# One loop body rewritten: 64x64 products gathered into three runs, a flip moved ahead, a first block of a sum changed

## The chip, the cores and the metric

The kernel runs on one core of a Trainium2 chip. A core has five engines with a queue each, which run side by side and wait for one another by semaphores: TensorE (PE in the profile; PEld is its weight load), VectorE (DVE), ScalarE (ACT), GpSimd (POOL) and SyncE (SP), which here only issues transfers. The metric is the device time of one execution in microseconds (us). Three executions of the kernel before took 638.33, 639.71 and 641.10 us; the median is 639.71 us.

## What is computed

The first block is a recurrent attention with 4 batches, 8 heads, 768 tokens and 40 dimensions of a head. Its state is a 40 by 40 matrix for each batch and head:

```
for t in range(S):
    y[:, :, t] = einsum('bhd,bhde->bhe', rt, state)
    Sa = einsum('bhde,bhe->bhd', state, at)
    state = state * wt - einsum('bhd,bhe->bhde', Sa, bt) + einsum('bhd,bhe->bhde', vt, kt)
```

Its output, as 3072 rows of 320, goes through the second block:

```
h = x @ w_in                                  # 320 -> 1024
sm = exp(h - max(h)) / (sum(exp(h - max(h))) + 1e-9)
solu = h * sm
ln = (solu - mean(solu)) / sqrt(var(solu) + 1e-6) * g_ln
out = ln @ w_out                              # 1024 -> 320
```

The attention's inputs are 32-bit floats. The three weights come as 64-bit floats, which the kernel reads as integers and takes apart on the chip.

## The kernel before

**Chunks.** The sequence is cut into chunks of 64 tokens. Two batches make a pair, so a step covers 2 x 64 tokens on 128 partitions; there are 2 pairs x 12 chunks = 24 such steps, numbered i. Within a chunk the recurrence is solved in closed form: a 64 by 64 triangular system for each head is inverted, and the rest is products.

**The products.** Most of them are 64 by 64 or smaller. They use a quarter of TensorE's array each: `half(p)` picks 64 rows and 64 columns, and `in_turn` deals the 16 products of a step (2 batches x 8 heads) over the four quarters. One name in the profile is 16 such products: `pu` (the solve), `pnt`, `pl`, `ps` (the scores, two runs of 16), `py`, `pz`, `px` (two runs), `pyo` (one run from the state, then 32 products of 104 columns). In 32-bit floats one product shows as two records. All go through the helper `mm`, so their line is L254 and one tells them by the tile's name. Between them stand full-width operations: transposes (`pa`, `pb`, `pk`, `pv`, `pr`, `pst`, `pei`, `plnT`), the running sum `pcum`, the product with w_in (`h`, six matmuls, two of them on 64 rows each) and the product with w_out (`po`, two groups of four).

**fence().** It is a TensorE drain: nothing is issued until all earlier products have ended. It stands where two row halves of the array would add into the same PSUM bank (within `px` and within `pyo`).

**The loop** (L785 to L843) runs i from -1. A pass does different things for different steps: step j = i + 5 gets its inputs scaled, transposed and multiplied (`front`, `norm`); step i + 1 gets its scores (`scores`), the coupling of its inverted blocks (`couple`, `close`); step i is solved and read out (`solved`, `answered`, `read`, `leave`); the second block works on steps i - 2, i - 3 and i - 4 (`hidden`, `exped`, `weighed`, `spreadof`, `folded`, `output`). The order in the text is the order in each engine's queue for PE, DVE, POOL and SP; only ScalarE's order is chosen by the scheduler.

**The inversion.** Every second pass two chunks' triangular blocks are inverted on VectorE in 30 steps of two instructions each (`prod`, then `uu`; L415 and L417). `some(n)` puts n of these steps at its place in the queue. The way there: `norm` writes `nt` to DRAM (POOL queue), four `blk` transfers bring it back in another layout (POOL queue), the steps run, the result `uu` goes to DRAM (SP queue), and `bring` fetches it as `tu` and `uh` (SP). `flip` transposes `tu` on VectorE; `py` needs that.

**Buffers.** PSUM tiles come from three pools. `banks` (two buffers of two banks) holds pu, ps, py, pnt, pl, pz, pyo, px in turn; `bank` (two buffers of one bank) holds the transposes, pcum, po and plnT in turn; `h` has one buffer. A tile that takes a buffer waits until its holder two places before has been copied out.

**The weights** are taken apart by `split`, in 13 parts: two VectorE instructions, three on ScalarE, then three on VectorE. `narrow(n, steps)` does n parts and spreads inversion steps between. Two parts come before the loop, the rest in passes -1 to 3. A pass 4 subtracts the mean from w_out (`centred`).

## Time and profile before

| | us |
|---|---|
| median of three executions | 639.71 |
| the profiled execution | 639.79 |
| its span, first to last instruction | 637.70 |
| TensorE busy | 567.5 (89%) |
| VectorE busy | 461.9 (72%) |
| GpSimd busy | 269.1 (42%) |
| ScalarE busy | 245.3 (38%) |
| start of pass 0 (its `px`) | 71.03 |
| start of pass 5 | 188.11 |
| start of pass 17 | 457.91 |
| end of pass 23's attention | 594.46 |

Passes 5 to 16 take 22.48 us each, pass 17 takes 21.95, pass 18 takes 21.37 and passes 19 to 22 take 19.78 each, from `px` to `px`. A busy time counts an instruction from its start to its modelled end, so for TensorE the distance from one start to the next is the better measure of what a piece costs. An idle time in brackets names what ended it. The chain of work that ended last gives PE 71% of the span and DVE 13%.

### The profile page before, as it was taken

How to read it: one execution, taken by the hardware profiler on the slowest of the kernel's cores; microseconds unless marked ns; L12 is line 12 of the kernel's file. 1: busy time of each engine (PE TensorE's matmuls, PEld its weight loads, DVE VectorE, ACT ScalarE, POOL GpSimd, SP SyncE). 2: the span in 40 equal slices, each digit the busy share in tenths (PEclk: the TensorE clock that was granted, in tenths of full speed). 3: DMA queues.
4: the chain of work that ended last, by engine and by line, in shares of the span. 5: the costliest groups of instructions: out<-in, count | busy, mean ns of one | idle time of the engine just before them, and what ended most of it. 6: DMA issues, size and time to landing. Idle time of an engine off the chain costs nothing.

```text
span 637.7 us, 26729 instructions
## 1 busy us (share of the span) xinstructions
PE 567.5 (89%) x11451; PEld 399.6 (63%) x11451; DVE 461.9 (72%) x1286; ACT 245.3 (38%) x498; POOL 269.1 (42%) x444
## 2 busy tenths in 40 slices
PE   5245677988999999999999999999999999999995
PEld 3134555756577677667667767666776666766653
DVE  4678799999878778778878777787887796443431
ACT  3412545554334434433443443344243333332221
POOL 3334345574274444445543642743544642222200
PEclk9665676688999999999999999999999999999998
DMA  8939896474355535544554553654423422210000
GB/s 166 159 73 169 170 164 131 107 152 87 71 110 93 111 87 95 107 93 103 103 120 79 108 116 73 119 107 95 91 53 70 98 49 49 51 36 26 24 20 21
DMA packets 217868, 59.92 MB, mean 94 GB/s; under 512 B 203216, under 2 KB 213048, under 8 KB 217752
## 3 DMA queue, kind: packets, MB, share of 16 engines
q1 hardware_dynamic: 200984, 34.47, 31.7%
q0 software_dynamic: 11376, 19.25, 12.6%
q10 hardware_dynamic: 5392, 4.51, 2.5%
q8 instruction: 90, 1.47, 1.0%
q14 instruction: 26, 0.21, 0.1%
HBM read 40.10 MB, written 13.37 MB: 84 GB/s over the span
## 4 chain that ended last, share of the span: by engine, by line
PE 71%; DVE 13%; DMA 6%; issue 4%; ACT 2%; SPq 2%; POOL 1%; DVEq 0%; ACTq 0%; POOLq 0%
PE h L254 16%; PE po L703 14%; PE pyo L254 7%; PE px L254 4%; PE pu L254 3%; DVE uu L417 3%; PE plnT L692 3%; PE ps L254 3%; DVE prod L415 3%; PE pl L254 2%; PE pr L334 2%; PE pnt L254 2%; PE pk L334 2%; PE pa L334 2%; PE pz L254 2%
## 5 line engine op out<-in xcount | busy, mean ns | idle before, releaser
L254 PE MATMUL h<-w_in,xT 128*128 128x512 f32 (+1 forms) x288 | 121.6, 614 | 0.0
L415 DVE TENSOR_TENSOR prod<-blk,uu 128x30 f32<-128x30 f32 (+4 forms) x360 | 99.0, 275 | 24.0 <-DMA blk<-nt_dram 14.0
L703 PE MATMUL po<-w,lnT 128*128 128x320 f32 x384 | 113.5, 440 | 0.0
L417 DVE TENSOR_TENSOR uu<-uu,prod 128x30 f32<-128x30 f32 (+4 forms) x360 | 101.9, 283 | 12.4
L703 PEld LDWEIGHTS po<-w,lnT 128*128 128x128 f32 x384 | 70.5, 190 | 29.3 <-issue 2.3
L655 DVE TENSOR_REDUCE nmax<-h 128x1 f32<-128x1024 f32 x24 | 29.4, 1224 | 60.0 <-PE h L254 59.9
L388 POOL DMA_DIRECT2D nt_dram<-nt x20 | 18.3, 916 | 119.0 <-DVE nt L362 97.7
L254 PEld LDWEIGHTS h<-w_in,xT 128*128 128x128 f32 (+1 forms) x288 | 38.9, 190 | 21.9 <-issue 20.8
L623 POOL TENSOR_TENSOR st<-tot,ex 104x160 f32<-104x160 f32 x44 | 22.1, 520 | 70.4 <-DVE tot L619 68.2
L681 POOL TENSOR_TENSOR rs<-c,mhalf 128x1 f32<-128x1 f32 x24 | 13.4, 559 | 91.0 <-DVE c L680 89.6
L635 POOL DMA_DIRECT2D xT<-x x96 | 48.7, 512 | 0.0
L254 PE MATMUL pyo<-lv,kb 64*64 64x104 f32 x768 | 38.6, 274 | 6.0 <-DVE lv L362 3.3
L693 ACT COPY lnT<-plnT 128x512 f32<-128x512 f32 x48 | 26.1, 589 | 43.3 <-PE plnT L692 43.3
L399 POOL DMA_DIRECT2D blk<-nt_dram x42 | 33.3, 800 | 13.0 <-DMA nt_dram<-nt 12.7
L658 ACT ACTIVATE e<-h,nmax 128x1024 f32<-128x1024 f32 x24 | 26.8, 1115 | 28.6 <-DVE nmax L655 27.5
L254 PE MATMUL pyo<-lu,kb 64*64 64x104 f32 x768 | 37.2, 266 | 0.0
L664 DVE TENSOR_TENSOR e<-h,e 128x1024 f32<-128x1024 f32 x24 | 29.4, 1225 | 10.1 <-ACT e L658 10.1
L276 POOL DMA_DIRECT2D raw_r<-in_r_dram x48 | 34.9, 729 | 0.3 <-issue 0.3
L672 DVE BATCH_NORM_STATS2 bs<-e 128x6 f32<-128x512 f32 x48 | 30.9, 686 | 0.8
L707 ACT ACTIVATE osb<-po,rs 128x320 f32<-128x320 f32 x24 | 12.7, 528 | 48.5 <-PE po L703 29.6
L254 PEld LDWEIGHTS pnt<-aT,bT 40*64 40x64 f32 x768 | 14.6, 144 | 26.5 <-issue 25.0
L254 PEld LDWEIGHTS pyo<-lv,kb 64*64 64x64 f32 x768 | 23.9, 145 | 11.3 <-issue 7.7
(130 smaller groups left out, 1127.0 us busy)
## 6 DMA issues: line engine op xcount, KB each, us to landing
blk<-nt_dram POOLq DMA_DIRECT2D x42, 128.0 KB, 4.2
nt_dram<-nt POOLq DMA_DIRECT2D x20, 256.0 KB, 3.5
raw_w<-in_w_dram SPq DMA_DIRECT2D x48, 80.0 KB
a<-in_a_dram SPq DMA_DIRECT2D x48, 80.0 KB
raw_r<-in_r_dram POOLq DMA_DIRECT2D x48, 80.0 KB, 3.3
lv<-in_v_dram SPq DMA_DIRECT2D x48, 80.0 KB
out_dram<-osb ACTq DMA_DIRECT2D x24, 160.0 KB
raw_b<-in_b_dram SPq DMA_DIRECT2D x44, 80.0 KB
```

Source lines behind the costliest of these rows:

```text
L254: nc.tensor.matmul(o, lhsT=lhsT, rhs=rhs, start=start, stop=stop, skip_group_check=True)
L276: queue.dma_start(out=x[half(p), :, 0:D], in_=ap[2 * bp + p, :, ci * C:(ci + 1) * C, :].rearrange("h t d -> t h d"))
L334: nc.tensor.transpose(out=t[0:W2, j * P:(j + 1) * P], in_=x[:, 2 * j:2 * j + 2].rearrange("p a b -> p (a b)")[:, 0:W2], identity=ident)
L399: queue.dma_start(out=nb[home:home + Q], in_=blocks[n][:, Q * e:Q * e + Q, Q * e:Q * e + Q])
L415: nc.vector.tensor_tensor(out=t, in0=nb[:, j:j + 1, j + 1:Q].to_broadcast([P, n_c, m]), in1=u[:, 0:n_c, j:j + 1].to_broadcast([P, n_c, m]) ...
L417: nc.vector.tensor_tensor(out=u[:, 0:n_c, j + 1:Q], in0=u[:, 0:n_c, j + 1:Q], in1=t, op=ALU.subtract)
L635: nc.gpsimd.dma_start(out=xT[to:to + Q, 2], in_=x[at + P - 3 * D:at + D, 2])
L655: nc.vector.tensor_reduce(out=nmax, in_=d["h"], axis=AX.X, op=ALU.max, negate=True)
L658: nc.scalar.activation(out=e, in_=d["h"], func=AF.Exp, bias=nmax, accum_out=d["esum"])
L664: nc.vector.tensor_tensor(out=d["e"], in0=d["h"], in1=d["e"], op=ALU.mult)
L672: nc.vector.bn_stats(out=bs[:, x], in_=d["e"][:, x * 512:x * 512 + 512])
L703: nc.tensor.matmul(d["out"][:, 0:DM], lhsT=d["lnT"][:, f, :], rhs=w2[:, f, :], start=f == 0, stop=f == NF - 1)
```

## The change

Nothing that is computed changes, and no product is added. The order of the loop body changes, with the buffer counts of two tiles.

- **Three runs.** TensorE's 64x64 products stand in three places of a pass: `pu, pu, ps, ps`; `py, pnt, pl`; and `pz, pyo, px` with the two 64-row matmuls of `h` in it. `scores(i + 1)` moves behind `solved(i)`, `couple` ahead of `norm` and `answered`, and `px` of step i + 1 (`carried`, `driven`) into the end of pass i, between and behind the parts of `pyo`. The transposes `pk`, `pv`, `pr` of step i + 2 move from the middle of pass i + 1 to the end of pass i; `pst` stays with step i.
- **One fence** stands where there were two: behind the own half of `pyo`, the state part of `px` and the 64-row matmuls.
- **The sum for h** begins with its third block (64 rows each) at the end of a pass and ends with the second block in the next, so that maximum and exponential (`exped`) follow it and `weighed` comes behind `answered`.
- **VectorE's order.** `flip` stands behind the maximum and ahead of `nt` and `lu`; before it stood behind `lu`. `psi` and `lv` move to the start of the pass. The inversion's 15 steps of a pass are split 3, 5, 3, 4 (before 3, 6, 0, 6), and in passes 0 to 3 4, 4 or 5, 3, 4.
- **GpSimd's order.** `by_value` moves ahead of the write of `nt`.
- **Before the loop** attention inputs of step 0 are transposed and scored early; `bring(0)`, `bring(1)` and `load_values(1)` are issued ahead of the weights' `land(3)`; the steps are split differently.
- `narrow` begins all its parts, runs the steps, then ends all parts. The tile `scale` gets two buffers, the tile `s` one in place of two.
- `centred` stands behind `decay`, just ahead of `output`.

```diff
@@ narrow @@
+        begun = []
         for x in range(n):
             load, part = next(parts)
-            rest = split(*part)
-            next(rest)
-            some(n_steps // n + (x < n_steps % n))
+            begun.append((load, part, split(*part)))
+            next(begun[-1][-1])
+        some(n_steps)
+        for load, part, rest in begun:
             for _ in rest:
                 pass
@@ driven @@
-        if d["opened"]:
-            fence()
@@ read @@
-        else:
-            fence()
@@ hidden @@
-            if (kt, x) == (0, 0):
+            if (kt, x) == (NK - 1, 0):
...
-               start=kt == 0, stop=kt == NK - 1)
+               start=kt == NK - 1, stop=kt == NK - 2)
@@ before the loop @@
         front(i)
+        front_b(i)
         decay(i + 1)
+        some(4 * (i > 1))
         norm(i)
...
-            some(8)
+            some(4)
...
     by_value(0)
+    attend_kv(0)
+    attend_r(0)
...
+    load_keys(6, "w")
+    some(10)
+    scores(0)
     decay(5)
-    load_keys(6, "w")
-    land(3, nc.sync)
-    some(14)
     load_keys(5, "ba")
-    load_values(1)
     bring(0)
     bring(1)
+    load_values(1)
+    land(3, nc.sync)
@@ the loop @@
-    shares = {-1: (0, 6, 2, 6), 0: (0, 6, 4, 6), 1: (0, 6, 3, 6), 2: (0, 6, 3, 6), 3: (0, 6, 3, 6)}
-    narrowed = {-1: (0, 1), 0: (1, 1), 1: (1, 2), 2: (1, 2), 3: (1, 1)}
+    shares = {-1: (0, 10, 2, 2), 0: (4, 5, 3, 4), 1: (4, 4, 3, 4), 2: (4, 4, 3, 4), 3: (4, 4, 3, 4)}
+    narrowed = {-1: (1, 0), 0: (1, 1), 1: (1, 2), 2: (1, 2), 3: (1, 1)}
...
-        pieces = shares.get(i, (3, 6, 0, 6))
+        pieces = shares.get(i, (3, 5, 3, 4))
```

The body of a pass after the change, whole:

```
        bring(i + 1); load_values(i + 2); some(pieces[0])
        solved(i); scores(i + 1)
        load_keys(j + 3, "w"); load_keys(j + 2, "bak")
        stated(i); front(j)
        hidden(m - 2, ((0, 1),)); narrow(some_weights[0], pieces[1])
        front_b(j); decay_turned(j + 1)
        hidden(m - 2, ((1, 1),)); exped(m - 2)
        scaled(j + 1); left(i - 1); by_value(i + 2); decay(j + 2)
        if i == 3 + LAG: centred(mean, 6)
        output(m - 3, 0)
        flip(i + 1); some(pieces[2]); couple(i + 1); norm(j); answered(i)
        weighed(m - 2); spreadof(m - 2)
        if ok(j) and j % GRP == GRP - 1: begin_inverse(j // GRP)
        output(m - 3, 1); narrow(some_weights[1], pieces[3])
        close(i + 1); read(i, True); carried(i + 1)
        if ok(m - 1): hidden(m - 1, ((2, 0), (2, 1)))
        fence(); read(i, False); driven(i + 1)
        leave(i); folded(m - 2)
        hidden(m - 1, ((0, 0),)); attend_kv(i + 2)
        hidden(m - 1, ((1, 0),)); attend_r(i + 2)
```

Here m = i - 1. `attend_r` and `stated` are the two halves of the former `attend_rs` (rT; pst and s), and `front_b` is the last line of the former `front` (pb and bT).

## The prediction

> **What bounds the kernel now.** I read the page's busy shares and slices first, then busy time by stage.
>
> ```profile
> PE 567.5 (89%) x11451; PEld 399.6 (63%) x11451; DVE 461.9 (72%) x1286; ACT 245.3 (38%) x498; POOL 269.1 (42%) x444
> ...
> PE   5245677988999999999999999999999999999995
> ...
> PEclk9665676688999999999999999999999999999998
> ```
> ```profile
> 71.03:188.11 117.08, 97.71 (x2186) 74.19 (x2182) 106.43 (x290) 53.79 (x114) 61.88 (x94) 0.84 0.63 123
> 188.11:457.91 269.80, 267.15 (x5785) 188.39 (x5784) 209.40 (x600) 110.96 (x227) 131.87 (x217) 1.00 0.50 100
> ```
> The second view has length, then busy PE, PEld, DVE, ACT, POOL, clock, DMA share, GB/s. Up to 188 us VectorE bounds (106.43 of 117.08 in passes 0 to 4). From 188.11 on PE does: 267.15 of 269.80, at full clock, and the waits list shows no wait of PE there. Twelve passes of 22.48 us are a pure sum of PE pieces. So the third view is PE's timeline of such a pass (start, length):
>
> ```profile
> 300.53 0.68 PE L254 MATMUL px<-st,aT 40*64 40x40 f32 x32
> 301.31 0.68 PE L254 MATMUL px<-lv,psi 64*64 64x40 f32 x32
> 301.92 0.65 PE L334 MATMUL pa<-cst,a 128*104 128x128 f32 x4
> ...
> 302.84 1.02 PE L254 MATMUL h<-w_in,xT 128*128 128x512 f32 x2
> 303.79 0.69 PE L254 MATMUL pu<-tu,x 64*64 64x64 f32 x32
> 304.31 0.63 PE L254 MATMUL pu<-x,tu 64*64 64x40 f32 x32
> 304.86 0.65 PE L334 MATMUL pk<-cst,kb 128*104 128x128 f32 x4
> ...
> 305.78 1.02 PE L254 MATMUL h<-w_in,xT 128*128 128x512 f32 x2
> 306.74 0.69 PE L254 MATMUL pnt<-aT,bT 40*64 40x64 f32 x32
> 307.36 0.64 PE L334 MATMUL pr<-cst,r 128*104 128x128 f32 x4
> ```
> Start to start, pnt alone takes 0.62 us, pu's two runs 1.07, and (in the same view) ps, ps, py 1.53: 0.46 a run, and about 0.16 left over for leaving the mode. An h matmul costs 0.86 before another h and 0.95 before a 64x64 run: 0.09 for entering. **A slot costs 0.25 us beside its runs.** The two px start 0.78 apart where pu's start 0.52 apart: the fence costs 0.26.
>
> [...] here runs of 32, 40 and 64 columns all cost about 0.46, so only entries, exits and fences can be saved. [...] I use starts. [...] the last blk packets land with the end of the output's transfer.
>
> **The change on PE, per pass.**
> - Slots: px, pu, pnt, pl, ps-ps-py, pz-pyo become three. 3 x 0.25 = 0.75 saved.
> - One fence fewer: 0.26 saved.
> - The 64-row matmuls: now 0.25 over their stream (pst to h 0.53 where pr to pst is 0.48; then 1.06 for 0.86), and pyo's fence costs 0.29 (0.47 where groups are 0.18 apart). Together 0.54. After, one exit (0.15), one drain behind h (0.2 to 0.35): 0.42 by choice, 0.12 saved (0 to 0.3).
> - Everything else is moved, not removed.
>
> Sum 1.13 us: 22.48 becomes 21.35 if no wait arises.
>
> **New waits.** I lay a pass out from plnT's start, T, with the steps of that view: plnT 0.93; h 0.85; pk, pv 0.48 and 0.44; h 0.85; pr 0.58 (with the entry); pu, pu, ps, ps 0.51, 0.47, 0.47, 0.62; pst, pa 0.46 each; h 0.85; pb, pei 0.48, 0.44; h 0.85; pcum 0.62; po 2.25; py, pnt, pl 0.51, 0.47, 0.62; po 2.35; pz, pyo from s 0.48, 0.49; own half 0.72; px 0.58; h64 with its drain 1.15; the other half 0.76; px 0.61. These sum to the 21.35. So pk starts at T+1.8, pu at 4.1, ps 5.1, pa 6.7, pei 8.5, pcum 9.7, po 10.4, py 12.6, pnt 13.1, pl 13.6, po 14.2, pz 16.6, px 18.3, h64 18.8. A copy starts about 0.06 after the modelled end of its last product. Durations on the other engines are the groups' means. Then each engine against it:
> - x0 (ACT 0.43) between px and pu: 4.1 us of cover, before 1.9. kT, vT, rT (0.6 each) finish at about T+4.9; ps needs rT at 5.6. Hidden; if ACT slipped over 0.7, PE would wait by the excess.
> - **flip to py.** VectorE: leave until T+0.9, steps, psi and lv at 5.9, aT at 7.4 (pa), five steps 3.05 to 11.1, maximum 1.23 to 12.3, flip 0.43 to 12.7. py could start at 12.6: about 0.2 lost.
> - **py to pl.** py and pl now share a `banks` buffer with only pnt between, so pl waits for wy. ScalarE runs the exponential (1.12 and 0.19) ahead of wy, and it waits for the maximum: 12.4 to 13.6, wy 0.47 to 14.1; pl could start at 13.8 after the late py: about 0.35 lost. Behind pl stand the second po, pz and pyo; all move with it.
> ```profile
> 292.71 0.47 ACT L454 ACTIVATE wy<-py,cst 128x256 f32<-128x256 f32 x1 [1.12 <-PE py L254]
> ```
>  Before, 2.4 us of po hid this.
> - **blk, every second pass.** nt is now made at about T+14.9 instead of 7.3 after px. On POOL the write of nt passes kb, the six xT transfers and by_value; none holds it, for nt is later than lv's landing (SP issues lv up to 10.6 after leave, landing near T+13.8). rs waits for VectorE until 18.8, so the blk issues run T+19.3 to 22.5.
> ```profile
> 270.91 3.17 POOL L399 DMA_DIRECT2D blk<-nt_dram  x4
> ```
> ```profile
> 280.27 0.19 DVE L415 TENSOR_TENSOR prod<-blk,uu 128x30 f32<-128x30 f32 x1 [1.77 <-DMA blk<-nt_dram]
> ```
>  Before, the last issue (273.3) lands 2 us before it is too late for anything but VectorE's own steps. After, it starts at about T'-0.2 of the next pass; the page's median of 4.2 us gives T'+4.0, the 6.9 seen above T'+6.7. Three steps (1.4) must end by psi's 5.9, so up to T'+4.4 costs nothing. I take 4.2, since the output's transfer, issued at T+17.7, is then over by T'+2.2; that pass loses about 0.3 (py to pl).
> - SP's order is kept: uu's write, xT, tu, uh, lv. tu was issued up to 7.2 us after leave (282.73 against 275.50), with some 2.5 us to land T+9.5; flip comes at 12.3. Hidden by 2.8; with less, flip and py wait by the excess.
> - POOL's state update stands behind blk until T'+0.6; its inputs come at T'+0.8. The h buffer: weighed ends at T+16.8, h64 wants it at 18.8. px's buffer, tu's copy: 17.9 against 18.3. Hidden by 2.0 and 0.4.
> - scale's second buffer and s's single one: no wait seen (s is read at the end of a pass, written near T+7).
>
> So two passes lose about 0.55 + 0.3, and with slowed steps 1.1: net saving per pass 1.13 - 0.55 = 0.58.
>
> **Sum.** Passes 5 to 17: 13 x 0.58 = 7.5. Pass 18: 0.8. Passes 19 to 22 have no pnt: five slots to three (0.50) + 0.26 + 0.12 = 0.88 each, 3.5. Pass 23: 0.5. Last 43 us: h64's fence costs 0.2 three times; the same time, since plnT's 0.23 wait goes: 0. Passes before 5 (VectorE): ScalarE waits in narrow (3.2 us) and psi's 3.45 go, but psi now stands behind pk, pv, pr and pu, where VectorE idles 2 to 4 us in each of five passes, against 10.7 idle in those passes now. centred's 2.9 us now stands ahead of po and flip (1.6 lost) where it already cost 1.42. I take 0, from 4 less to 5 more. Total 12.3: 639.79 - 12.3 = 627.5. The profiled execution lies 0.08 from the median, span 637.70 and 2.09 around it.
>
> **Rivals.**
> - *Waits give it back, no change (636.5 to 643).* VectorE's chain aT, steps, maximum, flip, py decides the pass when it slips by 0.6 more in each pass; e.g. POOL's kb and copies slow the steps (0.28 to 0.43 beside st at 299.5). For: VectorE is 209.40 of 269.80 and would be 84% of a shorter pass. Against: no wait of VectorE on PE is removed by it. 13 x 0.58 + 1 gone: about 639.
> - *Slower: blk late.* From T'+4.4 on each us of lateness holds psi, aT, maximum, flip and so py. The gain outside is 12.3 over some seven such passes, 1.8 each; it turns slower from T'+6.2, and at the 6.9 us landing plus the queue's own delay, T'+8, it loses 3.6 x 7 - 12.3 = 13: 652. For: 1.8 us of waits for blk stand already, and blk is issued 3 us later against leave. Against: the output's transfer ends earlier.
> - *Better: nothing waits and the start gains.* 1.13 x 13 + 4.8 + 4: 616. For: ScalarE idles 58%. Against: the py-pl buffer.
> - *The tail of slots is not the mode.* If joined runs keep their 0.16 and 0.09 [...], only 0.38 a pass is left, less the waits: 640. Against: pu-pu is 0.52.
>
> **Chances.** Forecast 0.58, better 0.12, waits even 0.12, slots keep their cost 0.03, slower 0.15. About 0.5% (3.2 us) is what a measurement can tell. The forecast's own range is 618 to 635. Eight in ten: better's 614 to the even case's 643; what is above (0.13 of the slower case) and below (0.05) is left out. Faster: 0.58 + 0.12 and a little of the even case, 0.72; same 0.11; slower 0.17.
>
> **What would show it.** PE's starts: pu to pu, pu to ps and ps to ps 0.47 apart; px to h64 near 0.6; h64 to pyo 1.1 to 1.2; px to px to px 21.6 to 22.1, alternating; waits of pl for wy near 0.4 and of py for flip near 0.2; prod waiting for blk until T'+4. Wrong if prod starts after T'+5, if passes 5 to 16 take over 22.3, or if pass 5 starts 5 us from 188.

## The result, and the profile after

The changed kernel takes 679.03 us (median of four executions, 676.63 to 684.43) against 639.8 us; the ratio is 1.063, with a 95% interval of 1.056 to 1.069. The forecast was 627.5 with a range of 614 to 643. The change made the kernel 6% slower where 2% faster was forecast, so the forecast is wrong in its sign. (Here and below, times are medians of all executions, while ratios and their intervals leave out an execution more than 1.5% above the fastest of its kernel, as one of four was in four of the experiments.)

The page of the kernel after, with the lines that answer to those of before (busy times, two rows of the slices, the chain by engine, and the median of a transfer's issue to its landing in the last column):

```profile
PE 564.9 (84%) x11451; PEld 411.3 (61%) x11451; DVE 469.2 (69%) x1286; ACT 248.4 (37%) x498; POOL 266.4 (39%) x444
...
PE   5164553875989999998998998989999998999995
...
PEclk9556567668889999999999999999999899999999
...
PE 52%; DVE 18%; DMA 12%; SPq 5%; ACT 5%; issue 4%; POOL 2%; ACTq 0%; DVEq 0%; POOLq 0%
...
blk<-nt_dram POOLq DMA_DIRECT2D x42, 128.0 KB, 5.9
```

TensorE's busy time is smaller than before (564.9 against 567.5 us), and yet the span is 38.8 us longer (676.5 against 637.7). The rows of nines have eights in them now, and TensorE's share of the last chain falls from 71% to 52%. The work did shrink; what grew are waits.

Busy time by stage of the kernel after, from pass 0's `pu` to pass 5's, and from there to pass 17's (length, then busy PE, PEld, DVE, ACT, POOL, the clock, DMA share, GB/s):

```profile
79.94:212.63 132.69, 98.74 (x2211) 77.01 (x2210) 102.48 (x273) 53.70 (x112) 57.46 (x93) 0.78 0.53 100
212.63:497.27 284.64, 266.02 (x5785) 194.75 (x5784) 218.23 (x601) 112.58 (x227) 132.41 (x217) 0.97 0.51 95
```

The same stretches took 117.46 and 269.81 before, the second with a clock of 1.00. With pass 0's `pu` at 79.94 in place of 73.91, this gives the whole account of the loss (us):

| stretch | before | after | loss |
|---|---|---|---|
| up to pass 0's pu | 73.91 | 79.94 | 6.0 |
| passes 0 to 4 | 117.46 | 132.69 | 15.2 |
| passes 5 to 16 | 269.81 | 284.64 | 14.8 |
| passes 17 to 22 | 121.64 | 124.90 | 3.3 |
| pass 23 and the end | 54.88 | 54.33 | -0.6 |

The rows don't hold quite the same work: `pk`, `pv` and `pr` of the next step now stand ahead of a pass's `pu`, so the first row has one set of them more than before (about 1.5 us of TensorE) and passes 17 to 22 have one less.

**An undisturbed pass.** TensorE's timeline of pass 16 of the kernel after (start, length):

```profile
475.58 0.69 PE L254 MATMUL pu<-tu,x 64*64 64x64 f32 x32
476.09 0.63 PE L254 MATMUL pu<-x,tu 64*64 64x40 f32 x32
476.53 0.67 PE L254 MATMUL ps<-aT,kT 40*64 40x64 f32 x32
477.02 0.65 PE L254 MATMUL ps<-rT,vT 40*64 40x64 f32 x32
477.60 0.65 PE L496 MATMUL pst<-cst,st 128*104 128x128 f32 x4
...
490.08 0.68 PE L254 MATMUL px<-st,aT 40*64 40x40 f32 x32
490.68 1.13 PE L254 MATMUL h<-w_in,xT 64*128 64x512 f32 x4
491.90 0.41 PE L254 MATMUL pyo<-lv,kb 64*64 64x104 f32 x8
```

The four runs start 0.51, 0.44 and 0.49 apart, and the way out costs 0.58. From this `pu` to the next is 21.70 us, against 22.48 before. So the gathering of the runs works, and is worth 0.78 us in a pass in which no long wait falls. Few passes are like that: the twelve take 25.1, 22.1, 23.8, 21.8, 25.7, 25.1, 26.2, 21.8, 23.9, 22.1, 25.4 and 21.7.

**The waits.** TensorE's list of waits between 188 and 620 us (what waited and for whom; us in all, times, longest). The kernel before has a single line in this stretch, 0.5 us of `plnT` in the last passes. The kernel after:

```profile
PE pl L254 <- ACT wy L460: 6.8, 5, 2.3
PE ps L254 <- issue: 5.6, 4, 2.0
PE pei L335 <- DVE aT L359: 4.5, 5, 1.3
PE py L254 <- DVE prod L421: 3.4, 2, 1.8
PE py L254 <- DVE tu L448: 2.9, 5, 1.4
PE po L709 <- DVE w L233: 2.2, 1, 2.2
```

The first line, on ScalarE's timeline of pass 11 (an odd pass, which begins a new inversion):

```profile
363.66 0.43 ACT L321 ACTIVATE inv<-pcum 128x320 f32<-128x320 f32 x1
366.85 0.47 ACT L316 ACTIVATE lw<-raw_w 128x320 f32<-128x320 f32 x1 [2.76 <-DMA raw_w<-in_w_dram]
367.23 1.10 ACT L664 ACTIVATE e<-h,nmax 128x1024 f32<-128x1024 f32 x1
...
368.31 0.46 ACT L460 ACTIVATE wy<-py,cst 128x256 f32<-128x256 f32 x1
```

`lw` is the logarithm for a later step. It waits 2.76 us for a transfer, and the exponential `e` and `wy` stand behind it in the queue. Before, the scheduler had `lw` behind `e`; there it waited 0.90 us in an odd pass, and `wy` behind it had to wait for TensorE's `py` anyway. TensorE in the same pass:

```profile
368.83 0.69 PE L254 MATMUL pl<-rT,nuT 40*64 40x64 f32 x32 [2.30 <-ACT wy L460]
369.46 4.00 PE L709 MATMUL po<-w,lnT 128*128 128x320 f32 x8
```

`pl` waits for 2.30 us, and then the second half of `po` takes 4.00 us where it takes 2.42 in pass 16. The clock is low behind the wait: 0.67 of it was granted in the 3.40 us from 369.00 on (below).

The third line, on VectorE in the same pass. Its `plnT` (T' of the forecast) starts at 352.05:

```profile
356.16 0.94 DVE L415 TENSOR_SCALAR uu<-blk 64x512 f32<-64x512 f32 x1 [2.40 <-DMA blk<-nt_dram]
...
358.03 0.19 DVE L421 TENSOR_TENSOR prod<-blk,uu 128x30 f32<-128x30 f32 x1 [0.79 <-DMA blk<-nt_dram]
```

The first `prod` starts at T'+5.98, and psi, aT, maximum and flip stand behind it.

The second line, "issue", is a wait for which the profile has no releaser. TensorE's timeline of pass 10:

```profile
332.49 0.63 PE L254 MATMUL ps<-rT,vT 40*64 40x64 f32 x26
334.67 0.34 PE L254 MATMUL ps<-rT,vT 40*64 40x64 f32 x6 [1.55 <-issue]
```

One run is cut in two by 1.55 us of nothing. It happens in passes 5, 10, 15 and 21. What the clock does behind the stall of pass 10 and behind the wait of pass 11, in stretches of the kernel after:

```profile
334.60:338.00 3.40, 3.33 (x19) 2.11 (x20) 2.87 (x6) 0.58 (x1) 1.75 (x3) 0.71 0.76 132
336.10:339.30 3.20, 3.20 (x11) 2.08 (x10) 2.96 (x10) 0.69 (x2) 1.30 (x2) 0.50 0.64 106
...
369.00:372.40 3.40, 3.40 (x39) 2.37 (x36) 2.77 (x4) 0.00 (x0) 0.09 (x1) 0.67 0.55 131
```

In the 3.4 us that follow, 0.71 and 0.67 of full clock was granted on average: the clock falls to 0.50 for 3.41 us, from 336.0 and from 370.1 on, and is back at 1.00 after that. In pass 11 the wait of 2.30 us so cost 3.88, with the 1.58 us more that `po` took. But the length of a pause alone does not decide it. In the kernel with `raw_w` early (below) the run `ps` of pass 15 stops for 2.64 us, and the clock behind it stays full:

```profile
437.24:440.64 3.40, 3.40 (x21) 2.48 (x21) 2.98 (x9) 1.43 (x3) 0.00 (x0) 1.00 0.51 78
```

The traces record the granted clock in stretches of 3.41 us, one after the other, and the low ones go with how much of a pause falls into one of them. In the kernel after, from 190 to 600 us, the three stretches at full clock in which TensorE stood for 2.21, 2.11 and 1.99 us (by the modelled ends) were each followed by a stretch at 0.50; so were four with 1.70, 1.55, 1.55 and 1.54 us, but not one with 1.25 us and none of 105 with less. In the kernel before, TensorE stood for less than 0.5 us in each of 121 stretches, and the clock stayed full. By my count over all kernels shown here, all 25 stretches with 1.9 us or more were followed by one at 0.50, of 79 with 1.2 to 1.9 us 33 were, and of 1864 with less, one. In the kernel after, the waits of `py` of 1.58 and 1.83 us behind 543 us lie across a border of two stretches each, with 0.96 us at most on one side, and the clock stays full. The pause of 2.64 us I read in the same way, with about 1.0 us ahead of a border and 1.7 behind.

**The start.** TensorE's waits between 60 and 205 us in the kernel after:

```profile
PE py L254 <- DVE tu L448: 28.6, 5, 8.4
PE pv L335 <- POOL v L308: 6.8, 1, 6.8
PE pz L254 <- DVE nt L368: 4.0, 3, 1.5
```

In each of passes -1 to 3 `py` waits 3.2 to 8.4 us for `flip` (line 448), which stands on VectorE behind the part of `narrow` and its steps. Ahead of pass 0's `pu` the longest wait is that of `pv`: `pv` of step 1 now stands in front of that `pu` and waits 6.78 us for GpSimd's copy of v, and VectorE, whose next piece is psi, is idle for 11.06 us. No run took this wait away, so it is not shown to be the 6.0 us of the first row.

### The profile page after: what moved, and what is told of

It is laid out like the page before. It is cut to its first block, busy times and chain, and to the rows that moved or that the text cites. A ratio compares the mean times of both kernels' runs of the same rounds, so it can differ in the third digit from the quotient of the medians.

```text
span 676.5 us, 26632 instructions
## 1 busy us (share of the span) xinstructions
PE 564.9 (84%) x11451; PEld 411.3 (61%) x11451; DVE 469.2 (69%) x1286; ACT 248.4 (37%) x498; POOL 266.4 (39%) x444
## 4 chain that ended last, share of the span: by engine, by line
PE 52%; DVE 18%; DMA 12%; SPq 5%; ACT 5%; issue 4%; POOL 2%; ACTq 0%; DVEq 0%; POOLq 0%
PE po L709 11%; PE h L254 10%; PE pyo L254 7%; DMA blk<-nt_dram 5%; DVE uu L423 4%; DVE prod L421 4%; DMA raw_w<-in_w_dram 4%; PE px L254 3%; PE pu L254 3%; PE plnT L698 3%; PE ps L254 3%; SPq L277 2%; PE pz L254 2%; PE pl L254 2%; DVE nmax L661 2%
## 5 line engine op out<-in xcount | busy, mean ns | idle before, releaser
L254 PE MATMUL h<-w_in,xT 128*128 128x512 f32 (+1 forms) x288 | 126.1, 622 | 0.0
L709 PE MATMUL po<-w,lnT 128*128 128x320 f32 x384 | 119.1, 457 | 2.7 <-DVE w L233 2.2
L423 DVE TENSOR_TENSOR uu<-uu,prod 128x30 f32<-128x30 f32 (+4 forms) x360 | 110.2, 306 | 12.4
L709 PEld LDWEIGHTS po<-w,lnT 128*128 128x128 f32 x384 | 74.1, 197 | 37.1 <-issue 7.9
L254 PE MATMUL py<-tu,nt 64*64 64x32 f32 x768 | 18.2, 237 | 35.2 <-DVE tu L448 31.6
L368 DVE TENSOR_TENSOR psi<-ps,cst 128x512 f32<-128x512 f32 x24 | 16.5, 688 | 42.7 <-PE ps L254 42.7
L254 PEld LDWEIGHTS py<-tu,nt 64*64 64x64 f32 x768 | 15.5, 152 | 47.5 <-DVE tu L448 40.1
L664 ACT ACTIVATE e<-h,nmax 128x1024 f32<-128x1024 f32 x24 | 26.6, 1110 | 39.8 <-DVE nmax L661 39.8
L405 POOL DMA_DIRECT2D blk<-nt_dram x42 | 33.3, 799 | 15.3 <-DMA nt_dram<-nt 15.0
L308 POOL COPY v<-lv 128x320 f32<-128x320 f32 x24 | 11.3, 471 | 70.2 <-DMA lv<-in_v_dram 70.2
L610 DVE TENSOR_TENSOR x<-pyo,ex 104x256 f32<-104x256 f32 x48 | 18.1, 419 | 29.1 <-PE pyo L254 29.1
L545 ACT COPY x<-px 128x320 f32<-128x320 f32 x24 | 10.2, 425 | 74.3 <-PE px L254 74.3
```

The lines of the kernel that those rows point to most:

```text
L254: nc.tensor.matmul(o, lhsT=lhsT, rhs=rhs, start=start, stop=stop, skip_group_check=True)
L405: queue.dma_start(out=nb[home:home + Q], in_=blocks[n][:, Q * e:Q * e + Q, Q * e:Q * e + Q])
L423: nc.vector.tensor_tensor(out=u[:, 0:n_c, j + 1:Q], in0=u[:, 0:n_c, j + 1:Q], in1=t, op=ALU.subtract)
L610: nc.vector.tensor_tensor(out=x[0:W2, 2 * q:2 * q + 2].rearrange("p g (b t) -> p b g t", b=2), in0=y[:, q, :, 0:C].rearrange("p (b g) c -> ...
L664: nc.scalar.activation(out=e, in_=d["h"], func=AF.Exp, bias=nmax, accum_out=d["esum"])
L709: nc.tensor.matmul(d["out"][:, 0:DM], lhsT=d["lnT"][:, f, :], rhs=w2[:, f, :], start=f == 0, stop=f == NF - 1)
```

## The experiments

The theories at the outset: **S**, the start is lost by the order of its passes; **F**, within it, by flip's place; **W**, the odd passes are lost by `lw`'s wait for `raw_w`; **B**, they are lost by the late `blk`; **I**, the stalls inside `ps` are waits for instructions. Median times below are of four executions unless said; the kernel before took 639.2 to 641.3 us beside them.

### raw_w earlier (W against B)

```diff
+        load_keys(j + 3, "w")
         if i >= 1:
             bring(i + 1)
...
-        load_keys(j + 3, "w")
         load_keys(j + 2, "bak")
```

> The changed kernel (679.0 us) with one transfer issued earlier: the load of raw_w stands at the top of a pass, ahead of bring and the values, in place of behind the scores. Theory W (ScalarE's lw, which now stands ahead of the exponential e, waits for raw_w in every second pass and holds e, wy and with them pl): pl's waits for wy (6.8 us in all between 188 and 620) fall below 2 and the six odd passes from 5 to 15 get about 1.5 to 3 us shorter each, lost clock included; 661 to 671. Theory B (the late blk alone makes the odd passes long): wy then waits for e behind the late chain anyway; 676 to 682. Neither expects the start (passes before 5) to move by more than 2 us.

Measured: 662.16 us, ratio to before 1.034 (1.029 to 1.039). TensorE's waits from 207 to 478 us in this kernel:

```profile
PE ps L254 <- issue: 6.6, 4, 2.6
PE pei L335 <- DVE aT L359: 3.1, 4, 1.0
PE py L254 <- DVE tu L448: 0.5, 2, 0.2
```

The line of `pl` and `wy` is gone; from pass 5 to 16 `lw` waits no more for `raw_w` (in the kernel after seven times, 10.8 us in all). The odd passes 5 to 15 take 22.5 to 24.4 us in place of 23.8 to 26.2, and passes 5 to 16 together 271.4 in place of 284.6: **13.2 us by one transfer's place in a queue.** W holds. B keeps a rest: odd passes without a stall take 22.5 to 22.7, undisturbed even ones 21.69. One part of the expectation failed: the start moved too, with pass 5's `pu` at 207.18 in place of 212.63.

### The first steps behind psi (B against W)

```diff
-        pieces = shares.get(i, (3, 5, 3, 4))
+        pieces = shares.get(i, (0, 5, 3, 7))
```

> The changed kernel with the three inversion steps at the head of a pass moved to its end from pass 4 on: 0, 5, 3, 7 in place of 3, 5, 3, 4. Theory B (in odd passes psi, aT, maximum and flip stand on VectorE behind the first steps, which wait for a late blk): psi follows the scores at once, pei no longer waits for aT, the odd passes get 2 to 3 us shorter; 662 to 668. Theory W (the wait of lw for raw_w makes the odd passes long, whatever VectorE does): 676 to 682. A third outcome: the seven steps at the end of a pass make uu late and tu with it, and the gain is given back in the next odd pass as a wait of py for flip; 674 to 684.

Measured: 686.01 us, ratio 1.068 (1.063 to 1.074): slower than the changed kernel, and outside all three expectations. The profiled execution, of 697.2 us, is the longest of the four, so its waits are given for their kind and not their size. psi now follows the scores at once, as B wanted, and `pei` no longer waits. But VectorE idles up to 6.6 us ahead of psi and then does the preparation of `uu` and five steps between psi and flip: from pass 5 on `py` waits for flip 16 times, 15.3 us in all, and `pl` for `wy` 8 times, 14.7 us. `tu` was not late; flip was, for what had been put ahead of it. In this loop, steps at the head of a pass use time in which VectorE waits for psi anyway, where their `blk` is there; steps between psi and flip delay `py`.

### The start of before, the loop of after (S)

Everything ahead of the loop and passes -1 to 4 in the order of the kernel before, from pass 5 on the changed body; at the end of pass 4 the parts of `px`, `h` and the transposes that the changed body expects.

```diff
     for i in range(-1, N + 3 + LAG):
+        if i < 5:
+            ...  # order, fences and steps of the kernel before
+            continue
```

> A kernel in two parts: everything before the loop and passes -1 to 4 in the order of the kernel before (two fences, psi at the end of a pass, flip behind lu, its narrow and its counts of scale and s), and from pass 5 on the changed loop body, the switch standing at the end of pass 4. Theory S (the 21 us lost before pass 5 are lost in the order of the changed passes -1 to 4 and its prologue, and the rest of the loss is a matter of the later passes alone): pass 5's pu starts near 192 as in the kernel before, the later passes take what they take in the changed kernel, 655 to 660. Rival (part of the start's loss is work that only moves: VectorE's backlog is met in passes 5 to 8): 663 to 672.

Measured: 656.22 us, ratio 1.022 (1.015 to 1.028). Busy time by stage, pass 0's pu to pass 5's and to pass 17's:

```profile
74.58:192.12 117.54, 99.22 (x2214) 75.32 (x2213) 103.85 (x284) 54.21 (x114) 63.01 (x97) 0.85 0.61 121
192.12:476.61 284.49, 266.21 (x5786) 194.64 (x5785) 215.88 (x598) 112.70 (x227) 132.79 (x217) 0.97 0.50 95
```

117.54 is the stretch of the kernel before (117.46), 284.49 that of the kernel after (284.64). The two losses stand side by side: S holds. The edit puts back everything about the start at once (the order, both fences, `narrow`, the buffer counts, the first block of the sum for `h`); two later experiments take the prologue and `narrow` apart from the rest.

### Flip ahead of narrow in the start (F)

```diff
+        if i < 4:
+            flip(i + 1)
         narrow(some_weights[0], pieces[1])
...
-        flip(i + 1)
+        if i >= 4:
+            flip(i + 1)
         some(pieces[2])
```

> The changed kernel with flip ahead of narrow and its steps in passes -1 to 3; passes from 4 on stay. Theory F (the start's loss is py waiting 28.7 us for flip behind narrow's part and four to ten steps): those waits fall below 8 us and pass 5 starts 8 to 14 us earlier; 665 to 671. Rival V (VectorE and the transfers bound the start; the steps and parts moved behind flip make the next psi late by as much): 675 to 682.

Measured: 665.76 us, ratio 1.038 (1.035 to 1.042), at the near edge of what F expected. The waits from 60 to 205 us:

```profile
PE pz L254 <- DVE nt L368: 13.5, 3, 5.3
PE py L254 <- DVE tu L448: 8.5, 2, 4.7
PE pl L254 <- ACT wy L460: 7.5, 4, 2.5
```

`py`'s waits fall from 28.6 to 8.5 us, but `pz`'s wait for `nt`, which now stands behind the steps, grows from 4.0 to 13.5, and `pl` waits 7.5 us for `wy`, where it did not wait before. Pass 5 starts 7.4 us earlier, not 8 to 14. Of the 20 us that `py` no longer waits, 17 come back at `pz` and `pl`.

### raw_w and flip together

```diff
+        load_keys(j + 3, "w")
         if i >= 1:
             bring(i + 1)
...
+        if i < 4:
+            flip(i + 1)
         narrow(some_weights[0], pieces[1])
```

> The changed kernel with raw_w loaded at the top of a pass and flip ahead of narrow in passes -1 to 3, both small edits together. Alone they gave 662.2 and 665.8 us. If they touch different waits (lw by raw_w in the odd passes, py by flip at the start), pass 5 starts at 198 to 202 us and the time is 652 to 657. If in the start both only reach the same bound (VectorE with transfers), pass 5 starts at 204 to 207 and the time is 657 to 662.

Measured: 665.35 us, ratio 1.039 (1.035 to 1.043); pass 5 starts at 206.77, the second case. In the start the two edits don't add: together they give no more than flip alone (205.28). The time is above both ranges; the profiled execution had 8.8 us of stalls inside `ps` from 190 us on.

### Step 5's k earlier in the prologue

```diff
     bring(1)
+    load_keys(5, "k")
     load_values(1)
     land(3, nc.sync)
-    load_keys(5, "k")
```

with flip ahead of narrow as above.

> The changed kernel with flip ahead of narrow in passes -1 to 3 (665.8 us), and with the load of step 5's k ahead of load_values(1) and of the weights' land(3). Theory K (in the prologue the load of k stands behind others, GpSimd's kb of step 5 waits 9.3 us for it, by_value(1) and pv stand behind that, 6.8 us, and psi of pass 0 after them): pv's wait falls below 2 us, pass 0 or 1 starts 3 to 6 us earlier; 659 to 663. Rival (the values or the half clock of the start take its place): 664 to 668.

Measured: 673.31 us, ratio 1.050 (1.045 to 1.054). `pv`'s wait for v is 6.0 us, as without it, and pass 0 starts at the same 79.44. The theory falls. In the profiled executions most of what it is slower than with flip alone comes after pass 5, in a loop whose code is the same (405.1 and 413.2 us from pass 5's pu to pass 23's); why is open. A difference of a few us between two kernels is therefore not yet the effect of an edit.

### The prologue and pass -1 of before

```diff
-    shares = {-1: (0, 10, 2, 2), 0: (4, 5, 3, 4),
+    shares = {-1: (0, 6, 2, 6), 0: (4, 5, 3, 4),
...
+        if i < 0:
+            ...  # the pass of the kernel before, with the end of the changed one
+            continue
```

(and the lines ahead of the loop as in the kernel before)

> The changed kernel with the prologue and pass -1 in the order of the kernel before, and the changed order from pass 0 on. Theory P (the prologue costs 6 us by itself, and what it leaves behind costs nothing in passes 0 to 4): pass 0's pu starts at 74 us and passes 0 to 4 take 132 us as in the changed kernel; pass 5 starts at 206, 671 to 675. Rival (passes 0 to 4 are long because the changed prologue brings values and k late): passes 0 to 4 take below 124 us; 660 to 668.

Measured: 672.23 us, ratio 1.050 (1.047 to 1.052). Pass 0's pu starts at 78.59 and passes 0 to 4 take 129.6. The time is where theory P had it, but by another sum: pass 0 starts 1.4 us earlier (`pv`'s wait is 2.8 us there), and passes 0 to 4 gain 3.1. `py` still waits 24.3 us for flip. So most of the loss is in the order of the passes, -1's tail included, and not in the prologue.

### The new narrow alone in the old start

```diff
-            rest = split(*part)
-            next(rest)
-            some(n_steps // n + (x < n_steps % n))
+            begun.append((load, part, split(*part)))
+            next(begun[-1][-1])
+        some(n_steps)
+        for load, part, rest in begun:
```

(with two buffers of `scale`) in the kernel with the start of before.

> The kernel with the order of before up to pass 4 and the changed loop from pass 5 on (656.2 us), but with the changed kernel's narrow, and two buffers of scale. If the order alone made the start long: pass 5's pu starts at 190 to 194 us, as with the narrow of before, and the time is 652 to 660. If narrow has a share: pass 5 starts at 197 or later, 663 or more.

Measured: 653.88 us, ratio 1.018 (1.012 to 1.025), pass 5 at 190.19. So the new form of narrow costs nothing that shows; what is left is the order of the passes, with their fences and the count of `s`, which no run takes apart.

### 128 more instructions (I)

```diff
+    t = bank("dummy")
+    for x in range(32):
+        mm(t[0:C, 0:C], cst[0:C, 0:C], cst[0:C, 0:C])
     decay(0)
```

> The kernel with raw_w loaded early (662.2 us), with 32 extra 64x64 products of the constant table ahead of the loop's prologue, whose result nobody reads: 128 more instructions in TensorE's stream, and nothing else. Theory I (the stalls of 1.3 to 2.9 us inside the second run of ps stand where a block of 256 TensorE instructions ends, and the next one, fetched as one 16 KB packet, is not there yet): a pass is about 968 instructions long, so a block's end moves by 56 in each pass, and 128 more put the stalls about 2.3 passes later: from passes 5, 10 and 15 to passes 7 or 8, 12 or 13 and 17. Rival (they belong to a transfer or an engine of these passes): they stay in 5, 10 and 15. The time stays between 657 and 668 either way.

Measured: 664.16 us (one execution). TensorE's timeline, the second halves of the interrupted runs in passes 7, 12 and 17:

```profile
256.48 0.46 PE L254 MATMUL ps<-rT,vT 40*64 40x64 f32 x16 [2.45 <-issue]
...
368.64 0.46 PE L254 MATMUL ps<-rT,vT 40*64 40x64 f32 x14 [0.41 <-issue]
...
481.60 0.45 PE L254 MATMUL ps<-rT,vT 40*64 40x64 f32 x12 [2.47 <-issue]
```

They moved from passes 5, 10 and 15 to 7, 12 and 17, by no other edit than the count. (Without it there are three more from pass 5 on, in passes 14, 19 and 21, and with it one more, in pass 20.) Passes 5, 10 and 15 now take 22.8, 21.7 and 22.6. I holds. The trace of the changed kernel says the same: counted over all of TensorE's records (matmuls, weight loads and its sequencer's), its four stalls begin at records 5569, 10433, 15297 and 20929, which are 19, 19 and 22 times 256 apart. All of them leave 193 when divided by 256, and so do, by my count, all the stalls inside `ps` of the kernel with `raw_w` early and of this one. TensorE's 22902 matmuls and weight loads go with 90 instruction packets of 16 KB on one queue, some 254 a packet. Around the stall of pass 10, an instruction packet of 16 KB starts at 332.15, takes 1.09 us, and the run goes on at 334.67, 2.5 us after the packet's start. In the kernel before, at least 3.15 us lie between a packet's start and the end of the block before it (from 188 us on); no stall occurs. Four runs in 2 us are 256 instructions (128 matmuls and 128 weight loads), as many as one whole block.

### Both mends, and flip in the last passes

The start of before with raw_w early, and then the same with `(3, 0, 8, 4)` steps from pass 18 on, so that none stands between psi and flip.

```diff
+        if i < 5:
+            ...  # order, fences and steps of the kernel before
+            continue
+        load_keys(j + 3, "w")
```

and, for the second,

```diff
-        pieces = (3, 5, 3, 4)
+        pieces = (3, 0, 8, 4) if i > 17 else (3, 5, 3, 4)
```

> The kernel in two parts (order of the kernel before up to pass 4, changed body from pass 5; 656.2 us) with raw_w loaded at the top of a pass from pass 5 on. If the loss of the start (21 us) and the loss by lw's wait for raw_w (about 12 us in passes 5 to 16) stand side by side, the two gains add: 192 us to pass 5, twelve passes at 21.7 to 23.0 with three stalls, and the rest as in the changed kernel; 641 to 648. If they overlap, the odd passes stay long for the late blk: 650 to 656.

> The same, and from pass 18 on the five steps of the inversion that stand ahead of flip stand behind it (0, 0... steps: none at the head or ahead of flip, 8 behind, 4 at the end). Theory F (in passes 18 to 22 TensorE waits 0.5 to 1.8 us for flip behind these steps, where less of its own work covers them): those waits are gone, passes 19 to 22 take 19.0 to 19.2 us where no stall falls, and the time falls by 4 to 6 us against the kernel without it. If flip waits for its transfer tu anyway: by less than 1.5 us.

Measured: 644.07 us (ratio 1.008, 1.005 to 1.010) and 641.88 us (20 executions from 638.92 to 646.82; 1.005, 1.003 to 1.007). The gains of S and W add up as the first expected. The second is 2.2 us faster, between its two cases and hardly clear of the spread: passes 20 and 21 take 19.8 each in place of 22.3 and 19.8, but pass 19 takes 24.6, with a wait of `py` of 2.6 us in it. The edit keeps three steps at the head of a pass, where the expectation says none; at them VectorE waits 5.6 us for `blk`, and psi and flip stand behind them.

### The first run broken

```diff
         solved(i)
-        if i >= 0:
-            scores(i + 1)
...
         front(j)
         hidden(m - 2, ((0, 1),))
+        if i >= 0:
+            scores(i + 1)
```

> The same as the last, with the first run broken in two: from pass 5 on, pst, pa and four matmuls of h stand between pu and ps. Theory I (a block of 256 instructions that lies in the one run pu, pu, ps, ps is used up in 2 us, faster than the next is fetched): the block now spans 4 us or more, the stalls inside ps are gone with the low clock behind them, some 3 to 4 us for each of five; the price is one more change between small and full products, 0.25 us in each of 19 passes, 4.7 us. Net 6 to 14 us faster than the last kernel. If the stalls have another cause they stay, and it is 3 to 6 us slower.

Measured: 660.65 us, ratio 1.032 (1.029 to 1.036): 19 us slower than the last, outside both expectations. TensorE's waits from 190 to 600 us, and its timeline in pass 8:

```profile
PE py L254 <- DVE tu L448: 16.3, 13, 1.7
```
```profile
272.95 0.67 PE L254 MATMUL py<-tu,nt 64*64 64x32 f32 x32 [1.58 <-DVE tu L448]
...
274.98 3.92 PE L714 MATMUL po<-w,lnT 128*128 128x320 f32 x8
```

The stalls inside `ps` are gone, as I says. But the scores start 2.94 us behind pu in place of 0.95, psi comes 2.0 and flip 1.4 to 1.8 us later, and `py` waits in 13 passes. In pass 8, behind a wait of 1.58 us, `po` takes 3.92 in place of 2.42. The even passes take 24.8 to 25.2 us, some 3.3 more than without the break; by the 1.50 us that `po` lost in pass 8, about half of that is clock (an estimate).

### blk ahead of rs (B)

```diff
+        if ok(j) and j % GRP == GRP - 1:
+            begin_inverse(j // GRP)
         weighed(m - 2)
         spreadof(m - 2)
-        if ok(j) and j % GRP == GRP - 1:
-            begin_inverse(j // GRP)
```

> The kernel with raw_w loaded early (662.2 us), with begin_inverse moved ahead of weighed and spreadof: the four blk transfers are issued behind the write of nt, and no longer behind rs on GpSimd. Theory B (what is left of the odd passes' length, 22.5 against 21.7 us, is the first steps on VectorE waiting for a late blk, with aT and pei behind them): blk is issued some 1 to 1.5 us earlier, pei's waits for aT (3.9 us in all from 207 us on) fall below 1.5, and the time falls by 3 to 6 us to 656 to 660. If the landing of nt decides when blk may start: within 1.5 us of the kernel without the move.

Measured: 661.34 us, ratio 1.033 (1.028 to 1.039), 0.8 below the kernel with raw_w early alone. On GpSimd the issue of blk now waits 38.5 us in all for the write of nt to land, against 14.7 without the move: that landing, not rs, decides when blk can start.

### Fewer steps ahead of flip

```diff
-        pieces = (3, 5, 3, 4)
+        pieces = (3, 1, 4, 7)
```

(the first with the run broken; the second with begin_inverse moved as in the experiment above too; the third with the run whole)

> The kernel of the start of before, raw_w early and the first run broken in two by pst, pa and four matmuls of h (660.7 us with the shares 3, 5, 3, 4), with the inversion's steps of a pass split 3, 1, 4, 7. There py waited 16.3 us for flip in 13 passes, up to 1.7 us at a time, and every such pass took 25 us. Theory F (flip stands behind psi, which the break makes 2.5 us later, and behind five steps of 0.6 us each): with one step there flip is 2.4 us earlier, the waits are gone, the passes from 5 to 16 take 21.9 to 22.5 us, no stall falls inside ps; 629 to 637. Rival (the seven steps at the end of a pass make uu and tu late, or psi's own lateness is enough): py goes on waiting over 8 us in all; 645 to 660.

> The same with begin_inverse ahead of weighed and spreadof, so that blk is issued ahead of rs. Theory B: the odd passes get 0.5 us shorter where blk still holds the first steps; 2 to 4 us below the last kernel. If psi's later place already covers blk: within 1.5 us of it.

> The kernel of 630.5 us (start of before, raw_w early, first run broken, steps 3, 1, 4, 7) with the first run whole again. Theory I (the block stalls cost about 2 us and the low clock behind them another 1 to 2, three to five times, against 4.7 us for one more change of products): three or more stalls inside ps are back; passes without a stall take 21.6 to 21.8; 634 to 642. Rival (the split of the steps alone did it and the break costs its 4.7 us): 625 to 629.

Measured: **630.48 us**, ratio 0.984 (0.981 to 0.987), 1.6% faster than the kernel before; with blk ahead of rs 630.06 (0.984, 0.981 to 0.987), no different; with the run whole again 633.98 (0.990, 0.986 to 0.994), at the edge of what I expected and above the rival. Busy time by stage of the first, from pass 5's pu to pass 17's and on to pass 23's:

```profile
191.23:455.01 263.78, 259.96 (x5786) 190.49 (x5785) 218.49 (x597) 110.81 (x227) 132.66 (x216) 1.00 0.56 102
455.01:574.08 119.07, 117.16 (x2689) 83.81 (x2688) 80.63 (x224) 43.42 (x85) 44.72 (x82) 1.00 0.30 60
```

The clock is 1.00 again, and the stretches are 6.0 and 2.6 us shorter than before's 269.81 and 121.64. Most passes take 21.8 us, odd ones among them. psi starts 4.2 us behind `pu` there, in place of 2.2, which gives a late `blk` more time; this fits theory B, but is no test of it alone. Of the way from 644.07, the steps gave 10.1 us and the break 3.5 more: without it four stalls, 4.4 us in all, are back. The break pays here, where flip no longer holds `py`; with five steps ahead of flip it cost 19 us.

### All mends in the changed order

raw_w early, flip ahead of narrow in the start, the broken run, and `(3, 1, 4, 7)` from pass 4 on, with the changed kernel's own prologue and passes -1 to 4.

```diff
-        pieces = shares.get(i, (3, 5, 3, 4))
+        pieces = shares.get(i, (3, 1, 4, 7))
...
+        load_keys(j + 3, "w")
...
         hidden(m - 2, ((0, 1),))
+        if i >= 0:
+            scores(i + 1)
+        if i < 4:
+            flip(i + 1)
         narrow(some_weights[0], pieces[1])
```

> The changed kernel, with its own prologue and its own passes -1 to 4, and four mends: raw_w early, flip ahead of narrow in passes -1 to 3, the first run broken by pst, pa and h, and the steps 3, 1, 4, 7 from pass 4 on. From pass 5 on it is the loop of the kernel of 630.5 us (437 us from pass 5's pu to the end); with a start of 198 to 207 us: 636 to 646. If the start is no shorter than in the changed kernel: 649 to 652.

Measured: 647.38 us, ratio 1.011 (1.008 to 1.013). From pass 5's pu to the end it takes 436.2 us, as expected; pass 5 starts at 210.1, later than either case had it, and the time lies between the two ranges. The loop is mended, the start is not.

## Why the prediction was wrong, step by step

Two terms of its sum made the forecast wrong: the passes before 5, taken as 0, lost 21 us, and the stretch from `py` to `pl`, taken as 0.35 us a pass, lost 13.2 us in passes 5 to 16 through a wait of `lw` that the working does not have.

- **Slots, fence and 64-row matmuls: right.** 21.70 us from pu to pu in an undisturbed pass, where 21.35 and 0.55 of waits were laid out; of the 0.35 above 21.35, 0.28 lie between `py` and `pl`. The starts are as forecast: pu to pu 0.51, ps to ps 0.49, px to h64 0.60, h64 to pyo 1.22. Behind the fence the next run starts 0.09 us after the modelled end of the last (`pyo` at 491.90, the 64-row matmuls from 490.68 for 1.13), where the runs of the first place overlap (`pu` 0.51 apart at 0.69). At 0.78 us in each of twelve passes the saving is 9.4 us (an estimate from the undisturbed passes), and the rival in which the slots keep their cost is excluded.
- **"py to pl, about 0.35": failed in the odd passes.** This step put the exponential right ahead of `wy` on ScalarE and never asked what else the scheduler would put ahead of the exponential. It was `lw`, which waits for the transfer of `raw_w` in the odd passes. `pl` waited up to 2.30 us a pass; with the low clock that is 13.2 us over passes 5 to 16, shown by the early load.
- **blk "T'+4.0, no loss": failed in size.** The issues lie where they were expected (349.3 to 352.5 us in front of pass 11, T'-2.7 to T'+0.5), but the median landing is 5.9 us where 4.2 was taken, and the first step starts at T'+5.98 in pass 11. The 4.2, the median before, was taken because the output's transfer would be over: in the kernel before, the last packets of the four `blk` issued from 270.91 on ended at 279.66 and the output's at 279.88. In front of pass 11 the output's ended at 353.21, T'+1.2, and `blk`'s at 356.97, so that end did not decide it here. The further 1.3 us of the queue's own delay in the slower rival were an estimate that no run shows. What is left in the odd passes once raw_w is early, some 0.8 to 1.0 us in each of six, about 5 us, comes with VectorE's waits for blk (26.6 us from 207 us on in that kernel) and `pei`'s for aT. No run took blk's lateness away alone, so this cause is argued. The rival with a late blk had the right sign, but at about 5 us it is smaller than the 9.4 saved and would not by itself have made the kernel slower.
- **flip to py, "about 0.2": right in passes 5 to 16 once lw is mended** (0.5 us in all). In passes 19 to 22 it failed: I took 0.88 us off each and did not lay them out. They have no pb, pei, pcum and pnt, so TensorE comes to `py` earlier, and it waited 1.58 and 1.83 us in the two passes after 543 us (the list of waits names `prod`, the instruction behind flip). There 0.81 us of TensorE's work is saved and twice that is waited.
- **"Passes before 5: I take 0, from 4 less to 5 more": failed, by 21 us, the largest term.** I counted VectorE's idle time ahead of psi and set it against waits that go. I did not lay the chain in line: psi, narrow's part, four to ten steps, flip, py, pnt, nt, and only then TensorE's way to the next psi. Both engines stood in turn: `py` waited 28.6 us, VectorE waited 12.4 us for psi between 60 and 212 us (11.06 of it once, with `pv`'s wait for v ahead of pass 0), while VectorE's busy time in passes 0 to 4 went down (104.96 to 102.48 us). The kernel with the start of before gave all of the 21 us back. How much of it is flip's place and how much that of `nt` and the maximum behind it stays open: the edit that helped one lengthened the others.
- **Unseen: instruction blocks and the clock.** Nothing in the working asked how fast TensorE's instructions arrive. The gathered run of 256 instructions in 2 us is what the change itself made. The spacing of the stalls gives blocks of 256, and where four runs used one up in 2 us, TensorE stood for up to 2.6 us. And each wait was priced at its length, where the low clock behind it could add more than half as much again (2.30 us and 1.58 of `po` in pass 11).
- **centred, 1.6 us:** 2.2 us of wait, and `po` behind it at low clock (0.50 from 196.06 to 199.47 us). **The tail, 0:** 0.6 us shorter.
- **Two sums of the prediction that don't come out.** In the rival without change, 13 x 0.58 + 1 gone leaves 3.8 of the 12.3 us, which is 636, not 639. And 209.40 us of VectorE are 80% of twelve passes of 21.90 us and 82% at 21.35, not 84%. Neither changes the forecast.

What the forecast named as its signs of being wrong came true: prod after T'+5, passes over 22.3 and pass 5 more than 5 us late. The account of passes 5 to 16 in one line: -9.4 for the slots, +13.2 for lw, and +11.0 left over, which I put down to the stalls inside ps and the late blk: 14.8 in sum.

## What to carry to other kernels

Before an engine is relieved, lay out one whole pass of every queue in order, ScalarE's as the scheduler orders it too, and ask at each instruction that waits for a transfer who stands behind it; do so again for the first and the last passes, where other work covers less. In a loop that TensorE bounds, ask what a wait costs through the clock behind it: here waits of 1.55 and 2.30 us had 3.41 us at half clock behind them, while others of 1.58, 1.83 and 2.64 us were followed by full clock. When small products are packed into long runs, count the instructions: here runs of 256 instructions in 2 us, one block by the spacing of the stalls, stood still for up to 2.6 us.

## What the runs showed of the hardware

- Some pauses of TensorE of 1.55 to 2.30 us were followed by 3.41 us at 0.50 of the clock (in the kernel after, behind the stalls of passes 5 and 10, 1.55 us each, and the wait of pass 11, 2.30 us). Behind that wait the second half of `po` took 4.00 us in place of 2.42; behind the wait of 1.58 us in pass 8 of the kernel with the broken run it took 3.92, with 0.75 of the clock granted in the 3.40 us from 272.95 on. In the kernel after, the clock fell in all three cases in which TensorE stood for 1.99 us or more within one recorded stretch of 3.41 us, and in four of five with 1.25 to 1.70 (over all kernels, by my count, in 25 of 25 with 1.9 or more and 33 of 79 with 1.2 to 1.9); behind the pause of 2.64 us of the kernel with `raw_w` early it stayed full.
- TensorE's instructions came in 16 KB packets (90 of them for 22902 matmuls and weight loads). Where four runs of 64, 256 instructions, were used up in 2 us, it stood for up to 2.6 us; all four such stalls of the kernel after lie whole multiples of 256 records apart. 128 added instructions moved stalls from passes 5, 10 and 15 to 7, 12 and 17.
- In the kernel after, three instructions of the inversion on VectorE that fell beside GpSimd's issue of raw_r and its two kb multiplies (328.8 to 332.0 us) took 0.97, 1.22 and 0.83 us in place of 0.29, 0.28 and 0.28 (the same shapes in the kernel before, from 300.43 us on). No run moved these, so that one slows the other is argued only.
